# Attention in chunks of 64 tokens, two to a unit, with the work on TensorE in 64x64 tiles

## The chip, the cores and the metric

One core of a Trainium2 chip. The metric is the device time of one execution in microseconds (us). Five engines work side by side on instructions in program order each: TensorE (PE; its weight loads are shown as PEld), VectorE (DVE), ScalarE (ACT), GpSimd (POOL) and SyncE (SP), which here only issues DMA transfers. They wait for each other by semaphores. Matmul results go to PSUM, which has eight banks of 2 KB a partition.

## The reference

A linear attention with a decaying state, then two feed-forward layers on its output:

```
B, H, S, D = 4, 8, 768, 48
state = zeros(B, H, D, D)
for t in range(S):
    cur = einsum('bhd,bhe->bhde', u * k_t, v_t)
    y_t = einsum('bhd,bhde->bhe', r_t, state + cur)
    state = w[:, None] * state + einsum('bhd,bhe->bhde', k_t, v_t)
x = y as (B * S, H * D)                        # 3072 x 384
x = (sigmoid(x @ w_gate) * (x @ w_val)) @ w_out       # inner width 1536
out = relu(x @ w_in)**2 @ w_out2                      # inner width 2048
```

## The kernel before

**Attention.** The 768 tokens are cut into 6 chunks of 128 (index c). A unit n is one chunk of one batch row b, so there are 24 units, n = 4c + b; "chunk 2" below is c = 2. In a unit, the scores of all pairs of tokens are made by matmul (`attn_scores`), from keys and queries that VectorE has multiplied by powers of w (`attn_prep`). `attn_diag` (ScalarE) writes the u term on the diagonal of a score tile `am`, and `attn_mask` (VectorE) copies the scores that count from PSUM into `am`. `attn_out` (TensorE) makes three things: the new contribution `pu` to the state (sums over tokens of scaled key times value; the keys are scaled by `attn_kh`, on GpSimd for c below 3, else on VectorE), the values times the masked scores, and, for c above 0, the state read by the queries. The last two add up in `ya` and `yb`; ScalarE copies them to SBUF, and DMA moves them on to be the input x of the layers. `attn_state` (VectorE) decays the state and adds the copy `us` of `pu`. All matmuls of the attention are fp32. A head has 48 columns, so four heads lie in two halves of the array: an output at PSUM partitions 0 or 64, and for the scores and state reads also an input at partitions 0 or 64.

**Order.** The order on each engine is the order in which the code calls. The four units of chunk 0 run first, while weights and inputs are loaded; `warm` puts matmuls without use between them and 24 behind them, which only keep TensorE busy. Then come the phases of the layers: layer 1 for chunk 0 (its first 7 of 12 inner tiles), for chunks 1 to 5, for the rest of chunk 0, and then layer 2. While layer 1 works on chunk c, the steps of the attention of chunk c+1 are called in between by `fill`, eight steps to a unit (`unit_ops`). So `attn_out` of unit n stands on TensorE between the products `pg` and `pv` of one inner tile, with the scores of unit n+1 at its end. The products are fp32r matmuls of 512 columns, three to one fp32 product. Weights come packed and are converted by ScalarE, VectorE and GpSimd (`convert`) during the first phases.

**Banks of PSUM.** `g` (pg), `v` (pv and also `yb`, which holds half of y and `pu`), `y` (`ya`), `a` (two, scores), `o` (two) and `o2` for the output of a layer.

Of the kernel before, what the change touches and what calls it, by code (L numbers as in the profile page):

```python
# [10 lines left out]
U8 = mybir.dt.uint8  # L11
# [9 lines left out]
C = 128  # L21
# [8 lines left out]
CENT = C // 2  # L30
# [11 lines left out]
def tile_kernel(  # L42
# [28 lines left out]
    anti = cp.tile([C, C], F32, name="anti")  # L71
    mask8 = cp.tile([C, C], U8, name="mask8")
# [3 lines left out]
    trk = cp.tile([DP, HP, C], F32, name="trk")  # L76
# [84 lines left out]
    def tables():  # L161

        R = 32
        e = sp.tile([DP, HP, C], F32, tag="xraw", name="e", bufs=1)
        d0 = sp.tile([DP, HP, R], F32, tag="sig", name="d0", bufs=2)
        d1 = sp.tile([DP, HP, R], F32, tag="sig", name="d1", bufs=2)
        px = cp.tile([DP, HP, 4], F32, name="px")
        f = lambda t: t.rearrange("p h n -> p (h n)")
        q = lambda j, n: px[:, :, j : j + 1].to_broadcast([DP, HP, n])
        pw = sp.tile([DP, HP, R], F32, tag="am", name="pw", bufs=2)  # L170
# [5 lines left out]
            out=f(pw), data0=f(d0), data1=f(d1), initial=0.0, op0=ALU.mult, op1=ALU.add  # L176
        )
        nc.scalar.copy(trk[:, :, CENT : CENT + R], pw)
        nc.vector.tensor_mul(px[:, :, 0], pw[:, :, R - 1], w_sb)
        nc.vector.tensor_mul(px[:, :, 1], px[:, :, 0], px[:, :, 0])  # L180
        nc.vector.reciprocal(px[:, :, 3], px[:, :, 1])
        nc.vector.tensor_mul(trk[:, :, CENT + R :], pw, q(0, R))
        nc.vector.tensor_mul(px[:, :, 2], px[:, :, 1], px[:, :, 1])
        nc.vector.tensor_mul(trk[:, :, 0:CENT], trk[:, :, CENT:], q(3, CENT))
        nc.vector.tensor_mul(e[:, :, 0:CENT], trk[:, :, CENT:], q(1, CENT))
        nc.vector.tensor_mul(e[:, :, CENT:], trk[:, :, CENT:], q(2, CENT))
# [53 lines left out]
    def attn_kh(n):  # L240

        if n >= NU or units[n][0] == NCH - 1:
            return
        k = kv_t[n][:, HD:]
        side(n).tensor_tensor(out=k, in0=k, in1=th, op=ALU.mult)

    def attn_scores(n):
        if n >= NU:
            return
        k, r = k_t[n], r_t[n]  # L250

        pa = pp.tile([C, 2, HP, C], F32, tag="o" if n < B and n % 2 else "a", name="pa")
# [13 lines left out]
        pa_t[n] = pa  # L266

    def attn_mask(n):
        if n >= NU:
            return  # L270
        am, pa = am_t[n].rearrange("p (j r) t -> p r j t", r=2), pa_t.pop(n)
        for p0, t0, t1 in ((0, 64, C), (64, 0, 64)):
            m = mask8[p0:C, t0:t1].unsqueeze(1).unsqueeze(1).to_broadcast([C - p0, 2, HP, t1 - t0])
            nc.vector.copy_predicated(am[p0:C, :, :, t0:t1], m, pa[p0:C, :, :, t0:t1])  # L274

    def attn_out(n):

        c, b = units[n]
        kv, am = kv_t[n], am_t.pop(n)
        ya = pp.tile([P, 2, C], F32, tag="y", name="ya")  # L280
        yb = pp.tile([P, 2 * C + HP * D], F32, tag="v", name="yb")
        pu = yb[:, 2 * C :].rearrange("p (j d) -> p j d", j=HP)
        py = [(yb[:, j // 2 * C : (j // 2 + 1) * C] if j % 2 else ya[:, j // 2]) for j in range(HP)]
        opened = set()

        def mm(out, q, m, bk, lhsT, rhs):

            nc.tensor.matmul(  # L288
                out[64 * q : 64 * q + m],
                lhsT=lhsT,  # L290
                rhs=rhs,
                start=(bk, q) not in opened,
                stop=True,
                skip_group_check=True,
            )
            opened.add((bk, q))


        width = (64, D)
        if c < NCH - 1:  # L300
            for h in range(H):
                q = h % 2
                mm(pu[:, h // 2], q, width[q], 1, kv[:, HD + h * D :][:, : width[q]], kv[:, h * D :][:, :D])
# [4 lines left out]
        if c:  # L308
            for j in range(HP):
                for q in range(2):  # L310
                    o = 64 * (head(q, j) % 2)
# [379 lines left out]
```

## Time and profile before

| | us |
|---|---|
| median of 3 runs | 979.89 (979.03 to 980.71) |
| the profiled execution | 980.53 |
| its span, first to last instruction | 978.7 |
| TensorE busy | 952.3 (97%) |
| VectorE, ScalarE, GpSimd busy | 454.4, 406.9, 128.5 |

The difference of 1.8 us between the execution and its span lies outside of what the trace shows. Busy is the time in which at least one instruction of the engine runs; matmuls overlap each other, so a busy TensorE can still be slow.

### The profile page before, as it was taken

Reading aid. Unit: us, or ns where it says so; the run is one execution under the profiler, and the core shown is the slowest. Engines: PE = TensorE matmul, PEld = TensorE weight load, DVE = VectorE, ACT = ScalarE, POOL = GpSimd, SP = SyncE. Lnnn points to the kernel's source line nnn. Section 1 sums busy time; section 2 is a strip of 40 time slices with the busy share of each in tenths; the row PEclk is TensorE's granted clock in tenths of the full one; section 3 lists DMA queues with packets and bytes.
Section 4 is the critical chain, followed back from the end, with each engine's and each line's share of the span. In section 5 each row is a group of like instructions: output and inputs, shape, how many; then the busy total and the mean of one; then the engine's idle time right before and its main releaser. Section 6 shows DMA issues by size and latency. Waiting matters only on the chain.

```text
span 978.7 us, 13895 instructions
## 1 busy us (share of the span) xinstructions
PE 952.3 (97%) x5544; PEld 758.0 (77%) x5544; DVE 454.4 (46%) x718; ACT 406.9 (42%) x802; POOL 128.5 (13%) x119
## 2 busy tenths in 40 slices
PE   7888999999999999999999999999999999999998
PEld 4566778878888888878888888888888888888886
DVE  7587677643355434323344364333433433433333
ACT  4667656633233234322466463332422322423322
POOL 5467533100000000000133121000000000000000
PEclk7899999999999999999999999999999999999999
DMA  8955554421214122001244440010000100100000
GB/s 309 290 161 156 159 166 149 139 84 54 78 34 137 52 61 85 7 7 37 93 128 128 162 129 1 1 65 1 32 33 1 65 1 1 64 1 1 33 1 32
DMA packets 42224, 76.74 MB, mean 78 GB/s; under 512 B 4912, under 2 KB 17584, under 8 KB 42160
## 3 DMA queue, kind: packets, MB, share of 16 engines
q1 hardware_dynamic: 42160, 75.87, 24.5%
q8 instruction: 43, 0.70, 0.3%
q14 instruction: 21, 0.17, 0.1%
HBM read 60.12 MB, written 11.01 MB: 73 GB/s over the span
## 4 chain that ended last, share of the span: by engine, by line
PE 88%; DVE 4%; ACT 3%; DMA 2%; issue 2%; POOL 1%; SPq 1%; DVEq 0%; ACTq 0%
PE pg L374 35%; PE po L393 19%; PE two L393 16%; PE pv L374 14%; PE ya L288 2%; PE yb L288 2%; DMA first<-in_rkv 1%; PE pa L256 1%; ACT am L238 1%; DVE first L222 1%; DVE raw L155 1%; ACT raw L153 1%; DVE am L274 1%; POOL wu L133 1%; ACT wu L132 0%
## 5 line engine op out<-in xcount | busy, mean ns | idle before, releaser
L374 PE MATMUL pg<-xh,wu 128*128 128x512 f32 x1008 | 316.6, 399 | 9.6 <-ACT xh L361 3.9
L374 PEld LDWEIGHTS pg<-xh,wu 128*128 128x128 f32 x1008 | 190.5, 189 | 58.9 <-ACT xh L361 4.8
L374 PE MATMUL pg<-xl,wu 128*128 128x512 f32 x504 | 195.6, 397 | 0.0
L521 ACT CAST gh<-s 128x512 fp32r<-128x512 f32 (+1 forms) x169 | 105.0, 621 | 207.7 <-DVE s L517 134.3
L393 PE MATMUL po<-gh,wu 128*128 128x512 f32 (+1 forms) x542 | 168.8, 392 | 0.0
L357 DVE TENSOR_TENSOR gl<-s,gh 128x512 fp32r<-128x512 f32 x162 | 114.2, 705 | 88.9 <-PE po L393 57.7
L520 DVE TENSOR_TENSOR s<-s 128x512 f32<-128x512 f32 (+1 forms) x97 | 66.6, 687 | 181.4 <-ACT s L519 181.4
L393 PE MATMUL two<-gh,wu 128*128 128x512 f32 x472 | 147.3, 393 | 0.0
L374 PE MATMUL pv<-xh,wu 128*128 128x512 f32 x432 | 138.4, 401 | 5.7 <-ACT ys L326 5.2
L519 ACT ACTIVATE s<-pg 128x512 f32<-128x512 f32 (+1 forms) x97 | 57.6, 594 | 190.3 <-PE pg L374 190.3
L517 DVE TENSOR_TENSOR s<-pv,s 128x512 f32<-128x512 f32 x72 | 49.7, 691 | 178.4 <-PE pv L374 177.3
L393 PEld LDWEIGHTS po<-gh,wu 128*128 128x128 f32 x542 | 101.6, 188 | 23.9
L374 PEld LDWEIGHTS pg<-xl,wu 128*128 128x128 f32 x504 | 95.4, 189 | 22.5
L393 PE MATMUL po<-gl,wu 128*128 128x512 f32 (+1 forms) x271 | 106.2, 392 | 0.0
L393 PEld LDWEIGHTS two<-gh,wu 128*128 128x128 f32 x472 | 88.5, 188 | 21.3
L374 PEld LDWEIGHTS pv<-xh,wu 128*128 128x128 f32 x432 | 79.5, 188 | 28.1 <-ACT ys L326 8.4
L393 PE MATMUL two<-gl,wu 128*128 128x512 f32 x236 | 92.4, 391 | 0.0
L503 ACT ACTIVATE s<-pg 128x512 f32<-128x512 f32 x72 | 44.0, 612 | 108.5 <-PE pg L374 108.5
L374 PE MATMUL pv<-xl,wu 128*128 128x512 f32 x216 | 84.9, 393 | 0.0
L153 ACT ACTIVATE raw<-raw 128x384 bf16<-128x384 bf16 x68 | 73.5, 1081 | 0.0
L238 ACT ACTIVATE am<-anti,dv 128x128 f32<-128x128 f32 x192 | 60.4, 391 | 15.5 <-DVE dv L228 15.5
L393 PEld LDWEIGHTS po<-gl,wu 128*128 128x128 f32 x271 | 50.8, 187 | 11.3
(295 smaller groups left out, 813.5 us busy)
## 6 DMA issues: line engine op xcount, KB each, us to landing
raw<-in_w SPq DMA_DIRECT2D x68, 384.0 KB, 3.1
kv<-in_rkv SPq DMA_DIRECT2D x16, 384.0 KB, 3.4
xin<-x2d SPq DMA_DIRECT2D x6, 768.0 KB, 4.2
out<-x2s SPq DMA_DIRECT2D x18, 256.0 KB, 2.0
first<-in_rkv SPq DMA_DIRECT2D x16, 256.0 KB, 6.0
kT<-in_rkv SPq DMA_DIRECT2D x16, 256.0 KB, 4.7
rT<-in_rkv SPq DMA_DIRECT2D x16, 256.0 KB, 5.2
x2d<-x2s SPq DMA_DIRECT2D x15, 256.0 KB, 2.0
```

The source lines that it names most:

```text
L133: nc.gpsimd.tensor_tensor(out=w[:, 1], in0=f1, in1=w[:, 0].bitcast(F32), op=ALU.subtract)
L153: nc.scalar.activation(top, top, AF.Prelu, scale=2.0**-112, alpha=2.0**32)
L238: nc.scalar.mul(am_t[n][:, h], anti, dv_t[n][:, h : h + 1])
L288: nc.tensor.matmul(out[64 * q : 64 * q + m], lhsT=lhsT, rhs=rhs, start=(bk, q) not in opened, stop=True, skip_group_check=True,)
L357: (eng or nc.vector).tensor_tensor(out=dst, in0=src, in1=high.bitcast(F32), op=ALU.subtract)
L374: nc.tensor.matmul(ps, lhsT=a, rhs=b_, start=(i == 0), stop=(i == len(pairs) - 1))
L393: nc.tensor.matmul(po[k][:, ts], lhsT=a, rhs=b_[:, ts], start=(first and m == 0), stop=(last and m == 2 and ts is cuts[-1]),)
L503: nc.scalar.activation(s, pg, AF.Sigmoid)
L517: nc.vector.tensor_tensor(out=s[:, ts], in0=pv[:, ts], in1=s[:, ts], op=ALU.mult)
L519: nc.scalar.activation(s[:, ts], pg[:, ts], AF.Relu)
L520: nc.vector.tensor_mul(s[:, ts], s[:, ts], s[:, ts])
L521: nc.scalar.copy(gh[:, ts], s[:, ts])
```

## The change

A unit still has 128 tokens, but they are two chunks of 64 (a = 0 and 1), one behind the other in the recurrence. Scores are made only within a chunk of 64, the state is carried from the first to the second chunk as `mid` (decayed, plus the sums of the first), and the decay tables (`trk`, `th`, `wdec`) are those of 64 tokens. Every matmul of the attention is one of 64 (or 48) rows, at most 64 columns of weights and at most 64 columns of data, so that the array holds four of them at a time. Each of the two heads and each of the two chunks has its own quarter.

The results stand in one tile `att` of three banks: the first and third hold y of the two chunks, the second and third the scores, and the sums stand beside them. Row halves of the array never write one bank at the same time; where the pairing of half and bank changes, `settle` puts a matmul of 8x8 in between. The bank `v` then holds only `pv` and the result of `settle`.

Sums for the state are made one unit ahead: `attn_out` of unit n now makes the values of n, the half of the reads of n whose bank fits, the scores of n+1, the sums of n+1 (`attn_sums`), and the other half of the reads. ScalarE copies the sums of n+1 (`attn_us`, two copies) and then y of n. Sums, `attn_kh` and `mid` are also made in the last chunk; the second half of the state after it is not. In chunk 0 the state was a copy; now it is decayed and added there too. In the start, scores of n+1 stood ahead of `attn_out` of n; now they are inside it.

```diff
-CENT = C // 2
+L = 64
+C = 2 * L
+CENT = L // 2
...
+    att = pp.tile([P, 3, 512], F32, name="att")
+    pa = att[:, 1:3, 0 : HP * L].rearrange("p r (j t) -> p r j t", j=HP)
+    y1, y2 = att[:, 0, 0 : HP * L], att[:, 2, HP * L :]
+    PU = HP * L
+    pu = [att[:, i, PU : PU + HP * D].rearrange("p (j d) -> p j d", j=HP) for i in (1, 0)]
...
+    opened = set()
+    def mm64(bank, q, out, lhsT, rhs):
+        nc.tensor.matmul(
+            out, lhsT=lhsT, rhs=rhs, start=(bank, q) not in opened, stop=True, skip_group_check=True
+        )
+        opened.add((bank, q))
+    def settle(x):
+        tok = pp.tile([P, T], F32, tag="v", name="tok")
+        nc.tensor.matmul(tok[0:8, 0:8], lhsT=x[0:D, 0:8], rhs=x[0:D, 0:8], start=True, stop=True)
     def attn_scores(n):
...
         for j in range(HP):
             for par in range(2):
-                x, z = (slice(64 * i, 64 * i + D) for i in (par, 1 - par))
-                nc.tensor.matmul(
-                    pa[64:C, par, j], lhsT=k[x, j, 64:C], rhs=r[x, j], start=True, stop=True
-                )
-                nc.tensor.matmul(
-                    pa[0:64, 1 - par, j, 64:C],
-                    lhsT=k[z, j, 0:64],
-                    rhs=r[z, j, 64:C],
-                    start=True,
-                    stop=True,
-                )
+                x = slice(64 * par, 64 * par + D)
+                for a in range(2):
+                    t = slice(a * L, (a + 1) * L)
+                    mm64(1 + par, a, pa[64 * a : 64 * a + L, par, j], k[x, j, t], r[x, j, t])
+    def attn_sums(n):
+        if n >= NU:
+            return
+        kv = kv_t[n]
+        settle(kv)
+        for j in range(HP):
+            for q in range(2):
+                h = 2 * j + q
+                for a in range(2):
+                    x = slice(a * L, (a + 1) * L)
+                    mm64(
+                        1 - a,
+                        q,
+                        pu[a][64 * q : 64 * q + width[q], j],
+                        kv[x, HD + h * D :][:, : width[q]],
+                        kv[x, h * D :][:, :D],
+                    )
     def attn_mask(n):
...
-        for p0, t0, t1 in ((0, 64, C), (64, 0, 64)):
-            m = mask8[p0:C, t0:t1].unsqueeze(1).unsqueeze(1).to_broadcast([C - p0, 2, HP, t1 - t0])
-            nc.vector.copy_predicated(am[p0:C, :, :, t0:t1], m, pa[p0:C, :, :, t0:t1])
+        m = mask8.unsqueeze(1).unsqueeze(1).to_broadcast([C, 2, HP, L])
+        nc.vector.copy_predicated(am, m, pa)
+    def attn_us(n):
...
+        us = us_t[n] = sp.tile([DP, 2, HP, D], F32, tag="us", name="us", bufs=2)
+        for a in range(1 if units[n][0] == NCH - 1 else 2):
+            nc.scalar.copy(us[:, a], pu[a][0:DP])
+        if units[n][0] == 0:
+            mid_t[n] = us[:, 0]
     def attn_out(n):
...
+        def reads(second):
+            for j in range(HP):
+                for q in range(2):
+                    h = head(q, j)
+                    a = h % 2 ^ second
+                    o = slice(64 * (h % 2), 64 * (h % 2) + D)
+                    if a or c:
+                        st = mid_t[n][o, j] if a else state[o, b, j]
+                        mm(a, q, j, D, st, r_t[n][o, j, a * L : (a + 1) * L])
         for j in range(HP):
             for q in range(2):
                 h = head(q, j)
-                mm(py[j], q, width[q], j % 2, kv[:, h * D :][:, : width[q]], am[:, h])
...
+                for a in range(2):
+                    x = slice(a * L, (a + 1) * L)
+                    mm(a, q, j, width[q], kv[x, h * D :][:, : width[q]], am[x, h])
+        reads(0)
+        settle(kv)
+        attn_scores(n + 1)
+        attn_sums(n + 1)
+        settle(kv)
+        reads(1)
...
+        attn_us(n + 1)
...
+    def attn_mid(n):
...
+        mid = mid_t[n] = sp.tile([DP, HP, D], F32, tag="mid", name="mid", bufs=2)
+        nc.vector.tensor_mul(mid, state[:, units[n][1]], decay)
+        nc.vector.tensor_add(mid, mid, us_t[n][:, 0])
...
             if late:
-                po[0] = pp.tile([P, T], F32, tag="y", name="po0")
+                po[0] = att[:, 0]
...
-                lambda n=n: attn_mask(n + 1),
+                lambda n=n: (attn_mask(n + 1), attn_mid(n + 1)),
...
         for n in range(B):
-            attn_scores(n + 1)
             attn_pre(n + 2)
             attn_prep(n + 2)
             warm(WARM_OUT[n])
             attn_out(n)
             attn_sum(n + 2)
             attn_mask(n + 1)
+            attn_mid(n + 1)
+            attn_state(n)
```

What this moves on TensorE, first in a unit of chunk 3, from the last matmul of the product pg to the first of pv. Before, with `yb<-kv` the sums, `ya<-am,kv` and `yb<-am,kv` values times scores, `rT,state` the reads, and `pa` the scores of the next unit:

```order
L374 MATMUL pg<-xl,wu 128x512
L288 MATMUL yb<-kv 64x48 [waits DMAHW0_49,DVE_49]
...
L288 MATMUL ya<-am,kv 64x128
L288 MATMUL ya<-am,kv 48x128
L288 MATMUL yb<-am,kv 64x128
...
L288 MATMUL ya<-rT,state 48x128 x2
L288 MATMUL yb<-rT,state 48x128 x2
...
L256 MATMUL pa<-rT,kT 64x128 [waits DMAHW7_49,DMAHW6_49,PE_49]
L259 MATMUL pa<-rT,kT 64x64
...
L374 MATMUL pv<-xh,wu 128x512 [waits PE_49,Activation_49]
```

The same place of the changed kernel, where `tok` is a settle and `att<-kv` a sum:

```order
L429 MATMUL pg<-xl,wu 128x512
L270 MATMUL att<-am,kv 64x64 x2
...
L270 MATMUL att<-rT,mid 48x64 x2
...
L278 MATMUL tok<-kv 8x8 [waits DVE_49]
L270 MATMUL att<-rT,kT 64x64 [waits DMAHW7_49,DMAHW6_49]
L270 MATMUL att<-rT,kT 64x64 x15
L278 MATMUL tok<-kv 8x8 [waits DMAHW4_49,PE_49]
L270 MATMUL att<-kv 64x48 [waits DVE_49]
...
L278 MATMUL tok<-kv 8x8 [waits PE_49]
L270 MATMUL att<-rT,mid 48x64
...
L429 MATMUL pv<-xh,wu 128x512 [waits PE_49]
```

The sums went from the head of the unit, where they were those of unit n, to behind the scores, where they are those of unit n+1; their wait for the engine that scales the keys (here VectorE) moved with them. The wait of pv for ScalarE is gone. Rows of one form that follow each other are counted (x2, x15).

On VectorE in the start, around the mask copy of unit 1 (`am<-mask,pa`) and the conversion of a weight tile behind it, before:

```order
L228 TENSOR_REDUCE dv<-first 128x8 [waits Pool_49]
L274 COPY_PREDICATED am<-mask_70,pa 128x2x4x64 [waits PE_49,Activation_49]
L274 COPY_PREDICATED am<-mask_70,pa 64x2x4x64
L145 SCALAR_TENSOR_TENSOR wt__328<-raw 128x384 [waits DVE_49,Activation_49]
L155 TENSOR_SCALAR raw<-raw 128x384 [waits DMAHW6_49]
```

and in the changed kernel:

```order
L245 TENSOR_REDUCE dv<-first 128x8 [waits Pool_49]
L319 COPY_PREDICATED am<-mask_70,att 128x2x4x64 [waits PE_49,Activation_49]
L397 TENSOR_TENSOR state<-us,wdec 112x192
L398 TENSOR_TENSOR state<-state,us 112x192 [waits DVE_49]
L146 SCALAR_TENSOR_TENSOR wt__376<-raw 128x384
L156 TENSOR_SCALAR raw<-raw 128x384 [waits DMAHW6_49]
```

One mask copy of the two is gone, and the decay and the add of the state of chunk 0 stand in its place.

## Rows read from the trace of the kernel before

**Rows 1.** Stages: span, busy us (x instructions) of PE, PEld, DVE, ACT, POOL; granted clock, DMA.
```profile
42.00:115.00 73.00, 62.31 (x506) 47.25 (x506) 55.13 (x78) 47.28 (x100) 43.54 (x35) 0.93 0.59 181
200.00:290.00 90.00, 90.00 (x655) 72.56 (x654) 41.17 (x72) 30.95 (x74) 0.00 (x0) 1.00 0.23 68
```

**Rows 2.** The chain that ended last, by engine, as shares of the span.
```profile
PE 88%; DVE 4%; ACT 3%; DMA 2%; issue 2%; POOL 1%; SPq 1%; DVEq 0%; ACTq 0%
```

**Rows 3.** TensorE's timeline in unit 14: start, us, what, [idle before].
```profile
241.64 0.39 PE L374 MATMUL pg<-xl,wu 128*128 128x512 f32 x1
241.96 0.61 PE L288 MATMUL yb<-kv 128*64 128x48 f32 x15
...
243.44 0.31 PE L288 MATMUL ya<-rT,state 48*48 48x128 f32 x2
...
243.59 0.28 PE L288 MATMUL ya<-rT,state 48*48 48x128 f32 x2
...
243.70 0.28 PE L288 MATMUL ya<-rT,state 48*48 48x128 f32 x2
...
243.91 0.22 PE L259 MATMUL pa<-rT,kT 48*64 48x64 f32 x1
243.92 0.27 PE L256 MATMUL pa<-rT,kT 48*64 48x128 f32 x1
243.93 0.22 PE L259 MATMUL pa<-rT,kT 48*64 48x64 f32 x1
243.93 0.27 PE L256 MATMUL pa<-rT,kT 48*64 48x128 f32 x1
243.97 0.28 PE L259 MATMUL pa<-rT,kT 48*64 48x64 f32 x3
...
244.58 0.39 PE L256 MATMUL pa<-rT,kT 48*64 48x128 f32 x4
244.90 0.73 PE L374 MATMUL pv<-xh,wu 128*128 128x512 f32 x2
```

**Rows 4.** TensorE's timeline around the first and the last unit of chunk 5.
```profile
379.29 0.86 PE L374 MATMUL pg<-xl,wu 128*128 128x512 f32 x3
...
382.55 0.73 PE L374 MATMUL pv<-xh,wu 128*128 128x512 f32 x2
...
438.00 0.39 PE L374 MATMUL pg<-xl,wu 128*128 128x512 f32 x1
...
440.48 0.73 PE L374 MATMUL pv<-xh,wu 128*128 128x512 f32 x2 [0.49 <-ACT ys L326]
```

**Rows 5.** Groups by line and shape, VectorE: busy us, mean ns | idle before.
```profile
L274 DVE COPY_PREDICATED am<-mask,pa 64x512 f32<-64x512 uint8 x24 | 17.9, 745 | 0.3
...
L342 DVE TENSOR_TENSOR state<-state,wdec 112x192 f32<-112x192 f32 x16 | 8.6, 537 | 0.0
...
L343 DVE TENSOR_TENSOR state<-state,us 112x192 f32<-112x192 f32 x16 | 6.4, 398 | 1.0
```

**Rows 6.** Timelines of TensorE and GpSimd in chunk 1 (42 to 115 us).
```profile
63.32 0.74 PE L374 MATMUL pv<-xh,wu 128*128 128x512 f32 x2 [1.90 <-ACT ys L326]
...
81.08 0.73 PE L374 MATMUL pv<-xh,wu 128*128 128x512 f32 x2
...
80.16 1.32 POOL L245 TENSOR_TENSOR first<-first,th 128x384 f32<-128x384 f32 x1
```

**Rows 7.** Timelines of ScalarE and TensorE in the start; two stages, columns as in rows 1.
```profile
22.24 0.39 ACT L327 COPY ys<-ya 112x256 f32<-112x256 f32 x1
...
32.49 5.35 PE L535 MATMUL pw<-idle 128*128 128x512 bf16 x24
41.70 3.12 PE L374 MATMUL pg<-xh,wu 128*128 128x512 f32 x6 [3.86 <-ACT xh L361]
...
41.28:48.11 6.83, 6.41 (x38) 4.83 (x40) 1.90 (x3) 2.01 (x4) 0.09 (x1) 0.50 0.97 328
91.60:94.05 2.45, 0.00 (x0) 0.00 (x1) 2.45 (x3) 2.45 (x7) 2.45 (x3) 1.00 0.21 30
```

More of the change, by code (lines that the diff above doesn't have):

```diff
@@ L75, in tile_kernel @@
     u_bc = cp.tile([C, H * D], F32, name="u_bc")
[L76 removed]
+    trk = cp.tile([DP, HP, L], F32, name="trk")
     th = cp.tile([C, H * D], F32, name="th")
@@ L175, in tables @@
         nc.vector.tensor_tensor_scan(
-            out=f(pw), data0=f(d0), data1=f(d1), initial=0.0, op0=ALU.mult, op1=ALU.add
+            out=f(p0), data0=f(d0), data1=f(d1), initial=0.0, op0=ALU.mult, op1=ALU.add
         )
-        nc.scalar.copy(trk[:, :, CENT : CENT + R], pw)
-        nc.vector.tensor_mul(px[:, :, 0], pw[:, :, R - 1], w_sb)
+        nc.scalar.copy(pw, p0)
+        nc.vector.tensor_mul(px[:, :, 0], p0[:, :, R - 1], w_sb)
+        nc.vector.reciprocal(px[:, :, 2], px[:, :, 0])
         nc.vector.tensor_mul(px[:, :, 1], px[:, :, 0], px[:, :, 0])
[L181 to L186, printed above, removed]
+        nc.vector.tensor_mul(trk[:, :, 0:CENT], p0, q(2))
+        for i in range(2):
+            pq = px[:, :, i : i + 1].unsqueeze(3).to_broadcast([DP, HP, 2, R])
+            nc.gpsimd.tensor_tensor(
+                out=e[:, :, :, i * R : (i + 1) * R], in0=twice(p0), in1=pq, op=ALU.mult
+            )
         return e, px
     def state_tables(e, px):
-        nc.gpsimd.tensor_copy(wdec, px[:, :, 2])
+        nc.gpsimd.tensor_copy(wdec, px[:, :, 1])
         for par in range(2):
-            pth = pp.tile([C, HP, D], F32, tag="gy"[par], name="pth")
+            pth = pp.tile([C, HP, D], F32, tag="gv"[par], name="pth")
             for j in range(HP):
@@ L279, in attn_out, with mm @@
         kv, am = kv_t[n], am_t.pop(n)
[L280 to L303, printed above, removed]
+        opened.clear()
+        def mm(a, q, j, m, lhsT, rhs):
+            mm64(2 * a, q, (y1, y2)[a][64 * q : 64 * q + m, j * L : (j + 1) * L], lhsT, rhs)
+        def reads(second):
[7 more added lines that the diff above has]
+                        mm(a, q, j, D, st, r_t[n][o, j, a * L : (a + 1) * L])
         for j in range(HP):
@@ L306, in attn_out @@
                 h = head(q, j)
-                mm(py[j], q, width[q], j % 2, kv[:, h * D :][:, : width[q]], am[:, h])
[L308 to L311, printed above, removed]
-                    mm(py[j], q, D, j % 2, state[o : o + D, b, j], r_t[n][o : o + D, j])
-            attn_scores(n + 1)
+                for a in range(2):
[7 more added lines that the diff above has]
+        reads(1)
         while len(kv_t) <= n + (4 if len(kv_t) < IN_W + 2 else 3) and len(kv_t) < NU:
             load_unit(len(kv_t))
+        attn_us(n + 1)
         if b == 0:
@@ L319, in attn_out @@
         ys = bank["y"]
-        if c == 0:
-            nc.scalar.copy(state[:, b], pu[0:DP])
-        elif c < NCH - 1:
-            us = us_t[n] = sp.tile([DP, HP, D], F32, tag="us", name="us", bufs=2)
-            nc.scalar.copy(us, pu[0:DP])
-        two = ys[0:DP, b].rearrange("p (i two) t -> p two i t", two=2)
-        nc.scalar.copy(two[:, 1], yb[0:DP, 0 : 2 * C].rearrange("p (i t) -> p i t", i=2))
-        nc.scalar.copy(two[:, 0], ya[0:DP])
+        for a, y in enumerate((y1, y2)):
+            nc.scalar.copy(ys[0:DP, b, :, a * L : (a + 1) * L], y[0:DP].rearrange("p (j t) -> p j t", j=HP))
         x = xraw[c]
@@ L335, in attn_out @@
             nc.sync.dma_start(out=x[96:128, 2], in_=ys[80:112, :, KT])
+    decay = wdec.unsqueeze(2).to_broadcast([DP, HP, D])
+    def attn_mid(n):
+        if n >= NU or units[n][0] == 0:
+            return
+        mid = mid_t[n] = sp.tile([DP, HP, D], F32, tag="mid", name="mid", bufs=2)
+        nc.vector.tensor_mul(mid, state[:, units[n][1]], decay)
+        nc.vector.tensor_add(mid, mid, us_t[n][:, 0])
     def attn_state(n):
-        b = units[n][1]
-        if n not in us_t:
+        c, b = units[n]
+        us, mid = us_t.pop(n), mid_t.pop(n)
+        if c == NCH - 1:
             return
         st = state[:, b]
-        nc.vector.tensor_mul(st, st, wdec.unsqueeze(2).to_broadcast([DP, HP, D]))
-        nc.vector.tensor_add(st, st, us_t.pop(n))
+        nc.vector.tensor_mul(st, mid, decay)
+        nc.vector.tensor_add(st, st, us[:, 1])
     xs = {}
```

56 lines of the change are left out of this document (33 added, 23 removed).

## The prediction

> **What bounds the kernel now.** I read the stages first, then the chain of work, then short stretches of TensorE's timeline. From 200 to 290 us TensorE is busy for all of the time at the full clock (90.00 of 90.00 us), while VectorE has 41 and ScalarE 31 us of work; from 42 to 115 us no engine is full and TensorE lacks 10.7 us of being busy [rows 1]. The chain that ended last is 88% TensorE [rows 2]. So there are two regimes. In chunks 2 to 5 of the attention (units 8 to 23, from about 115 us) every 0.1 us that a unit holds TensorE is 0.1 us of the run. Before that, VectorE, ScalarE, GpSimd and the DMA queue pass work to each other, and what counts is who is late for whom.
>
> **A unit on TensorE before.** The last projection matmul in front of a unit starts at 241.64, the first behind it (pv) at 244.90: 3.26 us [rows 3]. In it: sums for the state and values times masked scores from 241.96 (1.48), reads of the state from 243.44 (0.47), scores of the next unit from 243.91 (0.99). Each fp32 matmul shows as two passes. The spacings inside give the price of a pass in one tile of the array. The reads run in four 48x48 tiles with 128 columns, and their groups of four start 0.11 apart (243.59, 243.70). The scores of 64 columns (L259) start on one tile at 243.91, 243.97 and 244.03 (the last of its row of three: 243.97 + 0.28 - 0.22): 0.058 for a pass of 64. The last four 128-column passes of the scores end at 244.97, one lasts 0.27, so the last starts at 244.70; pv follows 0.20 later, where a pass takes 0.11: a change of tile shape costs 0.09. The change in front is inside the 0.32 from 241.64 to 241.96. The first pass behind a change has its weights unhidden: 0.15 to the second group of reads instead of 0.11, so 0.04.
>
> **A unit after.** 67 matmuls instead of 40, all but three in 64x64 tiles. Values times scores: 16 matmuls, 32 passes over four tiles, 8 x 0.058 = 0.46. Reads: 8 matmuls of 64 columns in two halves, 4 x 0.056 = 0.22 each (their weights are 48 wide, so I take two thousandths less). Scores and sums: 16 matmuls, 0.46 each. Three 8x8 matmuls (`settle`) lie between, another tile shape each time: out 0.09, two passes with some 0.04 together, in again 0.09, weights 0.04: 0.26 each. Such a matmul stands nowhere in the trace. Its bounds are 0.06 (no change of shape is felt, only two passes of 0.03) and 0.50 (the 0.20 in front of pv twice, and as much again as its passes); I take 0.26, made of the shape changes that the rows show. Sum: 0.32 + 0.04 + 0.46 + 0.22 + 0.26 + 0.46 + 0.26 + 0.46 + 0.26 + 0.22 + 0.09 = 3.05 against 3.26, **0.21 less in each of the 12 units of chunks 2 to 4: 2.5 us**. What the tiles win (1.48 to 0.92, 0.99 to 0.46) goes into the settles (0.78).
>
> In chunk 5 sums are now made too. A unit there took 2.79, from the third pass of its last row of pg (379.29 + 0.86 - 0.39 = 379.76) to pv at 382.55; it will take 3.05: +0.26 three times. The last unit took 2.48, of which 0.49 was pv waiting for ScalarE to empty the bank that y and pv share [rows 4]; with no next unit it takes 0.32 + 0.04 + 0.46 + 0.22 + 0.26 + 0.08 + 0.22 + 0.09 = 1.69, and pv's bank holds no y: -0.79. Together 0.
>
> A rule of the Trainium skill speaks against all this. "TensorE: Matmul & The Clock Gate" (section "Wait — 56ns, not 53.3ns?") says that with hardware decode off the sequencer spends about 62 ns on each MATMUL, which becomes the bound where the array work is shorter. By it the 67 matmuls would take 4.15 us, and the unit would be longer than now. The row of scores does not bear it out: seven passes start between 243.91 and 244.03, 0.020 apart, 0.040 a matmul [rows 3], though they may have been queued.
>
> **Other engines in the dense part.** VectorE loses the half-height mask copy (0.745 us, the second of two a unit) and gains a decay and an add for the middle state (0.537 + 0.398): +0.19 a unit [rows 5]. ScalarE copies the sums twice instead of once; its eight diagonals are half as wide. TensorE hides this while the two have half their time free [rows 1]; on a full engine it would cost the 0.2. ScalarE reaches y only at the end of the unit, 1 us later than now, but its next date is the cast behind pv, 2 us off.
>
> **Chunk 1, 42 to 115 us.** pv no longer waits for the copy of y (1.90 us at 63.32). But sums move up one unit, and with them the need for the scaled keys: GpSimd makes those of unit 7 from 80.16 to 81.48, while unit 6 holds TensorE and its pv starts at 81.08 [rows 6]. Now TensorE stands until 81.5 in front of those sums, and 0.46 + 0.26 + 0.22 + 0.09 follow: pv at 82.5, 1.4 us later. Queued behind on ScalarE are the copies of sums and y and two casts, for which GpSimd and then the next product wait. VectorE gets its mask copy earlier, since scores now end in the middle of a unit. A lost wait of 1.9, a new one of 1.4 and 0.19 more on VectorE per unit: I take 0 for all, bounds -2 (the old wait was on the path, the new one is not) and +3 (the new ones of two units are).
>
> **Prologue.** The DMA queue's next entry waits for y of unit 0, copied at 22.63 [rows 7], and later loads stand behind it. In the new order the values of unit 0 are followed by half its reads, a settle, scores, a settle, sums, a settle and the other reads, 2.4 us of which half was not ahead of y before: some 1.3 us late, and the loads with it. VectorE also decays and adds a state per unit that ScalarE copied before (0.94 less the mask's 0.745, four times: 0.8), and the order inside the unit puts scores behind values (some 0.8 in all). So I expect the first product 1.5 us late (43.2 for 41.70), and the 24 matmuls that only keep TensorE busy, behind the fourth unit, to start near 35.4 instead of 32.49. Their 5.35 us end near 40.8, and TensorE stands idle for 2.4 us, not 3.86. After the 3.86 the clock was at half from 41.28 to 48.11; in the 2.45 us idle before 94.05 it stayed full [rows 7]. If it falls as before, the product starts 1.5 us later and the scores of the unit behind it come 1.3 us earlier within the unit than before: 0 in the chain, which goes on with the mask copy.
>
> **Sum.** -2.5 in chunks 2 to 4, 0 in chunk 5, -0.1 for what chunk 1 passes on of its 0.21 a unit, 0 in the prologue: -2.6. On the profiled 980.53 us (span 978.7) that is 977.9; the median of the runs is 0.64 lower: **977.3 us**.
>
> **Rivals.**
> - *The clock stays full at 42 us.* Six of the first nine matmuls took 3.12 us at half clock [rows 7], so the nine about 4.4; half of that comes back, and 0.7 at the head of the unit behind; with the 1.3 by which its scores come earlier, less the late start of 1.5, the chain is 2.7 us earlier: 974.6. For: the shorter idle time. Against: my 2.4 is a difference of two estimates.
> - *Settles are dearer, or four tiles disturb each other, or the late keys of chunk 1 come through.* 47 settles lie on the path (36, 9 and 2). At 0.29 to 0.45 each: 979 to 986; it turns at 0.31.
> - *Settles are nearly free*, 0.06: 47 x 0.20 more, 968.
> - *TensorE is bound by its instructions.* Reads and scores took 0.47 and 0.99 for 8 and 16 matmuls, 0.059 and 0.062 each, whatever their tiles. If that is a rate of issue, small tiles win nothing: 67 x 0.058 + 0.41 = 4.3 a unit, +1.0 in 12 units, +1.5 in three, +3 in chunk 1: 1000. It turns at 0.042 a matmul. For: two unlike stretches agree. Against: 0.11 for each round of four reads is also what their columns give, and the 0.020 above. The rule quoted is this mechanism; by its 62 ns it would be 1004.
>
> **How the numbers follow.** Forecast 0.36, full clock 0.20, dearer settles or late keys 0.20, issue bound 0.16, free settles 0.05, none of them 0.03. A measurement of this kernel tells about 0.2% (2 us) from no change. Of the forecast's 0.36 I count 0.25 as faster, of the dearer case half within 2 us. Faster 0.25 + 0.20 + 0.05 = 0.50; the same 0.11 + 0.11 + 0.02 = 0.24; slower 0.09 + 0.16 + 0.01 = 0.26. The range leaves out the issue bound and part of the free settles: 970 to 987; the forecast's own is 975 to 980.
>
> **What would show it.** In a unit of chunk 3: 3.05 us from the last pg to the first pv, passes of one tile 0.058 apart, and a hole of 0.26 at each settle. Starts 0.03 apart throughout would be the issue bound. pv without a wait on ScalarE's y; sums with a wait on GpSimd near 80 us; y of unit 0 written 1.3 us later; granted clock between 41 and 48 us at half. TensorE idle behind 200 us would mean a wait that I missed.

## The result: 989.52 us, 0.98% slower, and where the time went

The changed kernel takes 989.52 us (median of 4 runs, 988.94 to 990.49), the kernel before 980.22 us beside it (4 runs, 979.03 to 980.71): ratio 1.0098, 95% interval 1.0080 to 1.0115. The forecast was 977.3 us, in a range from 970 to 987. It was wrong in sign and missed the range.

The profiled execution has a span of 988.7 us, some 10 more than before. The two stages of [rows 1] in the changed kernel, and its chain beside [rows 2]:

```profile
42.00:115.00 73.00, 63.24 (x708) 45.79 (x707) 53.04 (x81) 44.38 (x101) 42.62 (x34) 0.83 0.54 169
200.00:290.00 90.00, 90.00 (x872) 72.30 (x871) 40.51 (x75) 31.52 (x84) 0.00 (x0) 1.00 0.23 72
```

```profile
PE 90%; DVE 4%; ACT 2%; issue 1%; POOL 1%; DMA 1%; SPq 0%; DVEq 0%; ACTq 0%
```

TensorE is as full as before in the dense stage (200 to 290 us). The early stage (42 to 115 us) has a lower granted clock (0.83 for 0.93). A milestone that both traces have is the start of the last pg ahead of a unit's attention on TensorE:

| last pg ahead of | before | after | later by |
|---|---|---|---|
| unit 4 (end of the start) | 45.47 | 51.36 | 5.89 |
| unit 8 (end of chunk 1) | 115.69 | 126.55 | 10.86 |
| from unit 8 to the last matmul's end | 858.35 | 857.10 | -1.25 |

So the start loses 5.9 us, chunk 1 another 5.0 (75.19 us from unit 4 to unit 8 instead of 70.22), and the dense part gives 1.25 back; 0.3 lies behind the last matmul.

**The dense part** went the way that was forecast, by less. TensorE's timeline of unit 14, to be read beside [rows 3]:

```profile
251.44 0.39 PE L429 MATMUL pg<-xl,wu 128*128 128x512 f32 x1
251.76 0.68 PE L270 MATMUL att<-am,kv 64*64 64x64 f32 x32
252.26 0.22 PE L270 MATMUL att<-rT,state 48*48 48x64 f32 x1
...
252.43 0.21 PE L270 MATMUL att<-rT,state 48*48 48x64 f32 x1
...
252.59 0.20 PE L278 MATMUL tok<-kv 48*8 48x8 f32 x2
252.72 0.69 PE L270 MATMUL att<-rT,kT 48*64 48x64 f32 x32
253.35 0.20 PE L278 MATMUL tok<-kv 48*8 48x8 f32 x2
253.48 0.67 PE L270 MATMUL att<-kv 64*64 64x48 f32 x32
254.07 0.20 PE L278 MATMUL tok<-kv 48*8 48x8 f32 x2
...
254.57 0.50 PE L429 MATMUL pv<-xh,wu 128*128 128x512 f32 x1
```

From 251.44 to 254.57 it is 3.13 us (forecast 3.05, before 3.26). The 32 passes of values times scores take 0.50 (251.76 to 252.26), 0.031 for a matmul of two passes, so TensorE is not bound by its instructions. From the start of the last round of reads (252.43) to the first score it is 0.29, of which one round is 0.056.

**The start** shows what failed. TensorE and VectorE, with [idle before] and the releaser; then ScalarE's copies behind unit 0 and the clock of one stretch (columns as in rows 1):

```profile
24.56 0.68 PE L270 MATMUL att<-am,first 64*64 64x64 f32 x32 [0.55 <-DVE am L319]
...
27.37 0.61 PE L590 MATMUL pw<-idle 128*128 128x512 bf16 x2
30.30 1.12 PE L270 MATMUL att<-am,first 64*64 64x64 f32 x32 [2.33 <-DVE am L319]
...
34.85 1.04 PE L590 MATMUL pw<-idle 128*128 128x512 bf16 x2
36.91 1.12 PE L270 MATMUL att<-am,first 64*64 64x64 f32 x32 [1.02 <-DVE am L319]
...
49.42 1.64 PE L429 MATMUL pg<-xh,wu 128*128 128x512 f32 x6
```

```profile
23.78 0.73 DVE L319 COPY_PREDICATED am<-mask,att 128x512 f32<-128x512 uint8 x1 [2.91 <-ACT ys L370]
24.40 0.92 DVE L397 TENSOR_TENSOR state<-us,wdec 112x192 f32<-112x192 f32 x1
25.36 1.05 DVE L398 TENSOR_TENSOR state<-state,us 112x192 f32<-112x192 f32 x1
...
29.54 0.71 DVE L319 COPY_PREDICATED am<-mask,att 128x512 f32<-128x512 uint8 x1
...
36.13 0.72 DVE L319 COPY_PREDICATED am<-mask,att 128x512 f32<-128x512 uint8 x1 [3.59 <-ACT ys L370]
```

```profile
22.66 0.54 ACT L327 COPY us<-att 112x192 f32<-112x192 f32 x2 [4.23 <-PE att L270]
23.09 0.66 ACT L370 COPY ys<-att 112x256 f32<-112x256 f32 x2
```

```profile
29.40:46.46 17.06, 15.14 (x250) 9.83 (x251) 9.27 (x21) 9.85 (x36) 4.32 (x5) 0.50 0.72 232
```

Unit 0 ends on TensorE at 22.55. ScalarE copies the sums made in it and its y until 23.75. Only then, at 23.78, does VectorE start the mask copy of unit 1, whose scores were made inside unit 0; and only behind that copy does unit 1 start, at 24.56. In the code the second half of y (`y2`) and half of the scores (`pa`) share one PSUM bank, and half of the sums shares a bank with the other half. The page "PSUM — Partial Sum Buffer" of the Trainium skill (section "PSUM bank collisions raise a hardware error") says that two engines must not be in one bank at a time and that accesses are to be guarded by bank; the wait on `ys` fits such a guard. Run e3 below shows that it goes when the scores get banks (and a tile) of their own. So the units of chunk 0 run in a ring: TensorE's unit, ScalarE's copies, VectorE's mask (for unit 2 also what VectorE had queued ahead of it), TensorE's next unit. Before, scores stood ahead of the unit in banks of their own and the mask ran beside it. TensorE now stands idle 2.33 us ahead of unit 2, and from 29.40 to 46.46 the granted clock is 0.50, 1.2 GHz: units 2 and 3 take 4.55 us (30.30 to 34.85, 36.91 to 41.46), unit 1 at the full clock 2.81 (24.56 to 27.37). The first product comes at 49.42 instead of 41.70 [rows 7].

**Chunk 1.** What TensorE waited for in all, from 46 to 126 us, how often, and the longest:

```profile
PE pg L429 <- ACT wu L133: 3.7, 3, 2.8
PE att L270 <- POOL first L262: 2.6, 2, 1.4
PE att L270 <- POOL kv L262: 2.3, 1, 2.3
PE pg L429 <- POOL wu L134: 1.9, 3, 0.8
PE pv L429 <- POOL wu L134: 0.4, 1, 0.4
```

The wait of pv for ScalarE's y [rows 6] is gone. Before, it took this much in the same stretch of the kernel:

```profile
PE pv L374 <- ACT ys L326: 4.4, 2, 2.5
```

In its place stand 4.9 us in which the sums wait for the keys that GpSimd scales (L262). The mask waits for y's copy here too. But the waits as such do not add up to the 5.0 us. From unit 4 to unit 8, first before, then in the changed kernel (columns as in rows 1):

```profile
45.47:115.69 70.22, 59.53 (x501) 45.35 (x500) 54.24 (x76) 46.59 (x98) 43.54 (x35) 0.96 0.56 172
51.36:126.55 75.19, 64.27 (x718) 49.18 (x717) 53.78 (x80) 46.08 (x102) 43.96 (x35) 0.86 0.52 161
```

TensorE stands idle for 10.7 and 10.9 us of this; what grew is its busy time, by 4.7, at a lower mean clock. The granted clock was at half (1.2 GHz) from 60.12 to 66.94, from 70.35 to 73.77, from 90.84 to 94.25 and from 101.08 to 107.91, 20.5 us in all, against 6.1 before. Each time it fell within a wait of TensorE or up to 2 us behind one: 2.8 us for converted weights, then 1.15, 1.4 and 2.3 us for keys. No run holds the clock up in this stretch of the changed kernel, so how much of the 5.0 us it made is not shown.

### The profile page after: what moved, and what is told of

Same layout as the page of the kernel before. It is cut to its first block, busy times and chain, and to the rows that moved or that the text cites. A ratio compares the mean times of both kernels' runs of the same rounds, so it can differ in the third digit from the quotient of the medians.

```text
span 988.7 us, 16639 instructions
## 1 busy us (share of the span) xinstructions
PE 961.3 (97%) x6904; PEld 764.3 (77%) x6904; DVE 453.1 (46%) x742; ACT 401.8 (41%) x826; POOL 135.0 (14%) x121
## 4 chain that ended last, share of the span: by engine, by line
PE 90%; DVE 4%; ACT 2%; issue 1%; POOL 1%; DMA 1%; SPq 0%; DVEq 0%; ACTq 0%
PE pg L429 34%; PE two L448 16%; PE pv L429 14%; PE po L448 11%; PE att L448 7%; PE att L270 5%; PE pw L590 1%; PE tok L278 1%; DVE first L239 1%; DMA first<-in_rkv 1%; DVE am L319 1%; ACT am L255 1%; POOL wu L134 0%; DVE raw L156 0%; DVE mid L388 0%
## 5 line engine op out<-in xcount | busy, mean ns | idle before, releaser
L429 PE MATMUL pv<-xh,wu 128*128 128x512 f32 x432 | 141.2, 408 | 0.4 <-POOL wu L134 0.4
L448 PE MATMUL po<-gh,wu 128*128 128x512 f32 (+1 forms) x338 | 105.5, 392 | 0.0
L448 PEld LDWEIGHTS po<-gh,wu 128*128 128x128 f32 x338 | 63.4, 188 | 14.6
L448 PE MATMUL po<-gl,wu 128*128 128x512 f32 (+1 forms) x169 | 66.2, 392 | 0.0
L448 PE MATMUL att<-gh,wu 128*128 128x512 f32 (+1 forms) x204 | 63.4, 392 | 0.0
L255 ACT ACTIVATE am<-anti,dv 128x64 f32<-128x64 f32 x192 | 50.1, 340 | 16.5 <-DVE dv L245 16.5
```

Source lines behind the costliest of these rows:

```text
L255: nc.scalar.mul(am_t[n][:, h], anti, dv_t[n][:, h : h + 1])
L429: nc.tensor.matmul(ps, lhsT=a, rhs=b_, start=(i == 0), stop=(i == len(pairs) - 1))
L448: nc.tensor.matmul(po[k][:, ts], lhsT=a, rhs=b_[:, ts], start=(first and m == 0), stop=(last and m == 2 and ts is cuts[-1]),)
```

## Experiments

Each kernel ran beside the kernel before (979.6 to 980.0 us, and 980.2 beside the changed kernel), on several chips. Gains in the text are differences of medians; by the ratios they differ by up to 0.7 us. The intervals of e1 to e4 overlap that of the changed kernel, those of e1 and e4 most: these two gains alone are not clear of noise. "Unit 4" is the start of the last pg ahead of it, "4 to 8" the stretch to the one ahead of unit 8, both from the profiled execution. Up to unit 3, e6, e9 and e12 are the same code (they differ first in `mid` of unit 4), and yet the first matmul behind unit 3 starts at 33.27, 34.62 and 34.26: one profile's start scatters by over a microsecond. From unit 4 on e8 and e11 are the same code, and their stretches differ by 1.6 us. So both columns count only together with the medians.

| kernel | median us | ratio to before, 95% | unit 4 | 4 to 8 |
|---|---|---|---|---|
| changed kernel | 989.52 | 1.0098 (1.0080 to 1.0115) | 51.36 | 75.19 |
| e1 mask first | 987.41 | 1.0084 (1.0069 to 1.0099) | 51.01 | 72.97 |
| e2 more warm | 986.55 | 1.0074 (1.0059 to 1.0089) | 47.90 | 74.51 |
| e3 scores ahead | 986.43 | 1.0069 (1.0052 to 1.0086) | 47.02 | 76.25 |
| e4 keys early | 988.31 | 1.0082 (1.0067 to 1.0097) | 51.44 | 73.79 |
| e5 settles 64x64 | 977.23 | 0.9973 (0.9963 to 0.9982) | 45.83 | 75.02 |
| e6 = e3 + e4 | 983.94 | 1.0036 (1.0023 to 1.0049) | 45.65 | 72.63 |
| e9 = e6, no mid in chunk 1 | 982.09 | 1.0018 (1.0008 to 1.0027) | 47.67 | 70.50 |
| e12 = e6, mid twice in chunk 1 | 986.68 | 1.0067 (1.0054 to 1.0081) | 49.06 | 75.54 |
| e7 = e6 + e5 | 974.21 | 0.9938 (0.9921 to 0.9954) | 47.58 | 71.92 |
| e8 = e7 + e1 | 974.13 | 0.9937 (0.9923 to 0.9952) | 46.03 | 73.38 |
| e10 = e7, more warm | 973.63 | 0.9933 (0.9918 to 0.9949) | 45.86 | 71.66 |
| e11 = e8, more warm | 973.96 | 0.9937 (0.9923 to 0.9952) | 46.89 | 71.76 |

**e1, the mask ahead of ScalarE's copies.**

```diff
         reads(1)
...
+        attn_mask(n + 1)
         attn_us(n + 1)
...
-                lambda n=n: (attn_mask(n + 1), attn_mid(n + 1)),
+                lambda n=n: attn_mid(n + 1),
...
             attn_sum(n + 2)
-            attn_mask(n + 1)
```

> The only edit to the changed kernel: the mask copy of unit n+1 (VectorE) is called in front of ScalarE's copies of sums and y instead of behind them. Theory (wait): the mask waits for the copy of y because half of y lies in a PSUM bank with half of the scores; without it the mask starts at the end of the unit on TensorE, 1.3 us earlier in each of the units 0 to 7 (for unit 4: 54.6 instead of 55.9 us), VectorE's 21.9 us of idle time in front of the mask ahead of 126 us fall by about 9, and the run becomes 5 to 7 us faster, 983 to 985. Rival (order): what costs is that the scores stand inside the unit at all; then the mask still comes behind the whole unit and the gain is under 2 us, 988 or more. Rival (exchange): sums and y are now copied behind the mask, 0.75 us later, and the next unit or the DMA of y waits for them instead: 989 to 991.

Groups of VectorE ahead of 126 us (busy, mean ns | idle before, releaser): first the changed kernel, then e1.

```profile
L319 DVE COPY_PREDICATED am<-mask,att 128x512 f32<-128x512 uint8 x9 | 6.6, 731 | 21.9 <-ACT ys L370 21.9
```

```profile
L319 DVE COPY_PREDICATED am<-mask,att 128x512 f32<-128x512 uint8 x9 | 6.6, 730 | 18.1 <-PE att L270 18.1
```

And ScalarE's copies in e1, behind unit 0:

```profile
23.57 0.54 ACT L327 COPY us<-att 112x192 f32<-112x192 f32 x2 [6.18 <-DVE am L319]
```

Mask and copies only read these banks, and yet whichever is called second waits for the other: the guard works both ways. The wait on y is gone and the mask now waits for TensorE alone, but the idle time falls by 3.8 us, not 9, and the run by 2.1. In the start nothing is won (51.01): the mask still follows the whole unit, as the rival said, and now y is copied behind the mask. In chunk 1 the stretch is 2.2 us shorter. So the wait for y's copy is real (the trace shows it go), but in the start it is only one piece of the ring.

**e2, the clock.** More matmuls without use between the units:

```diff
-    WARM0, WARM_OUT, WARM_X = 13, (8, 6, 2, 2), 24
+    WARM0, WARM_OUT, WARM_X = 13, (8, 10, 14, 10), 34
```

> The changed kernel with more of the matmuls that only keep TensorE busy in the start: 10, 14 and 10 instead of 6, 2 and 2 in front of units 1 to 3, and 34 instead of 24 behind unit 3. Nothing else moves. Theory (clock): TensorE idles 2.3 and 1.0 us in front of units 2 and 3, and the clock is at half from 29.40 to 46.46 us for it; filled, it stays full there, units 2 and 3 take 2.7 instead of 4.3 us and the first product starts some 3 us earlier: 985 to 986.5. Theory (wait): the loop of mask, unit and copy of y sets the time whatever the clock; units 2 and 3 become shorter only if the clock stays up, and without that the time is that of the changed kernel, 989 to 990. Rival: the matmuls that were added stand in front of units that are ready, and cost up to 2 us: 990 to 992.

TensorE and its clock from 22 to 47 us in e2:

```profile
22.00:47.00 25.00, 24.85 (x430) 14.66 (x429) 18.42 (x31) 17.21 (x56) 14.02 (x12) 1.00 0.77 237
```

The clock stays full and every unit of the start takes 3.11 us from the matmul ahead of it to the one behind. The run is 3.0 us faster and unit 4 comes 3.5 us earlier, though the masks still wait for y's copy in this kernel. So a little more than half of the 5.9 us of the start was paid through the clock: the ring made the idle time, the idle time was followed by 1.2 GHz, and that made the ring itself longer.

**e3, the scores where they stood before the change**, for units 1 to 4, in the free banks `o`:

```diff
+        pa, at = att[:, 1:3], 1
+        if 0 < n <= B:
+            pa, at = pp.tile([P, 2, 512], F32, tag="o", name="pa"), f"o{n}"
...
-        attn_scores(n + 1)
+        if c:
+            attn_scores(n + 1)
...
+            attn_scores(n + 1)
             attn_out(n)
```

> The changed kernel with the scores of units 1 to 4 in front of attn_out of the unit before, as they stood before the change, in the two banks `o` that are free in the start; later units as in the changed kernel. Theory (wait): the mask of unit n+1 then runs beside unit n instead of behind it and behind its y; TensorE no longer waits 2.3 and 1.0 us for masks in chunk 0, its last pg ahead of unit 4 comes near 46 instead of 51.36 us, and the run becomes 5 to 6 us faster, 983 to 985; what chunk 1 loses (5 us between units 4 and 8) stays. Rival (VectorE): the decay and add of the state in chunk 0, about 0.9 us a unit, set the start, and little is won: 988 or more.

VectorE's masks of units 2 to 4:

```profile
25.53 0.74 DVE L325 COPY_PREDICATED am<-mask,pa 128x512 f32<-128x512 uint8 x1 [0.76 <-ACT am L255]
...
29.71 0.73 DVE L325 COPY_PREDICATED am<-mask,pa 128x512 f32<-128x512 uint8 x1 [0.45 <-ACT am L255]
...
35.70 0.71 DVE L325 COPY_PREDICATED am<-mask,pa 128x512 f32<-128x512 uint8 x1
```

No mask of the start waits for y any more: with banks of their own for the scores the wait is gone. Unit 4 comes 4.3 us earlier, the run is 3.1 us faster, less than the 5 to 6 expected. In the profile, 1.1 of what the start won is lost again in chunk 1. The edit does two things at once, banks of their own and scores ahead of the unit; banks of their own with the order kept were not run.

**e4, the keys scaled early.**

```diff
-                lambda n=n: (attn_state(n), attn_pre(n + 2)),
+                lambda n=n: (attn_state(n), attn_pre(n + 2), attn_kh(n + 2)),
...
-                lambda n=n: attn_kh(n + 2),
+                lambda: None,
```

> The changed kernel with GpSimd's scaling of the keys of unit n+2 called directly behind its other two operations for that unit, four steps earlier, from unit 4 on; in the start all stays. Theory (keys): in chunk 1 the sums of unit n+1 wait on TensorE for these keys (4.9 us in the profile of the changed kernel, in units 5, 6 and 7), since GpSimd reaches them behind four or five other operations. Called early they are there in time, the three units fall from 5.50, 4.63 and 6.19 to 3.2 to 3.5 us, and the stretch from unit 4 to unit 8 from 75.2 to 71 or 72 (before the change 70.2): 985 to 987. Rival (converted weights): chunk 1 is bound by the conversion of the weights on ScalarE, VectorE and GpSimd; 1.3 us of GpSimd moved ahead of a conversion only move the wait from the sums to pg or pv, and the stretch stays within 1 us: 988.5 to 990.

TensorE's waits in the same stretch, 46 to 126 us, in e4:

```profile
PE pv L429 <- POOL wu L134: 4.0, 4, 1.6
PE pv L429 <- ACT wu L133: 3.1, 2, 1.6
PE pg L429 <- POOL wu L134: 1.7, 3, 0.8
```

The wait for the keys is gone (4.9 us), and pv now waits 7.1 us for converted weights instead of 0.4. The three units are 3.13 us long, yet the stretch wins only 1.4 and the run 1.2. The mean clock of the stretch is 0.88, little more than 0.86. Both theories said something true: TensorE waited 4.9 us for the late keys, and about a quarter of that reaches the end, since the weights are due next.

**e5, settles that keep the tile shape.**

```diff
-    def settle(x):
+    def settle(x, q=0):
...
-        nc.tensor.matmul(tok[0:8, 0:8], lhsT=x[0:D, 0:8], rhs=x[0:D, 0:8], start=True, stop=True)
+        z = slice(64 * q, 64 * q + 64)
+        nc.tensor.matmul(tok[0:64, 0:8], lhsT=x[z, 0:64], rhs=x[z, 0:8], start=True, stop=True)
...
-        settle(kv)
+        settle(kv, 1)
         for j in range(HP):
```

> The changed kernel with its three settles a unit made as matmuls of a 64x64 tile (64 rows, 64 columns of weights, 8 columns of data) instead of 48x8, so that the tile shape does not change in front of and behind them; each still waits for the one before. Theory (shape): a settle costs 0.26 to 0.29 us because the shape changes twice; it falls to 0.06 to 0.1, so a unit of chunks 2 to 5 takes 2.5 to 2.6 instead of 3.13 us and the run is 8 to 10 us faster, 979.5 to 981.5. Rival (drain): the cost is the ordering itself, whatever the shape, and the unit stays at 3.1 us: 989 to 990.

TensorE around the first settle of a unit of chunk 3 in e5:

```profile
243.10 0.21 PE L270 MATMUL att<-rT,mid 48*48 48x64 f32 x1
243.15 0.17 PE L279 MATMUL tok<-kv 64*64 64x8 f32 x1
243.16 0.28 PE L270 MATMUL att<-rT,kT 48*64 48x64 f32 x3
```

Reads, settle and scores now follow each other without a hole, and the unit takes 2.53 us instead of 3.13: 0.20 less for each settle, 9.0 us in 15 units. The run is 12.3 us faster than the changed kernel (8 to 10 were expected), and faster than before. "TensorEngine Tiling (Array Packing)" of the Trainium skill ("Key Properties") says that a change of tiling mode drains TensorE; this agrees. The first score now starts 0.01 us behind the settle, so the 0.20 us is the price here of two changes of shape together with the emptying of the array between them, which the run does not take apart. The other 3 us go with the start (unit 4 at 45.83), where each unit is a link of the ring and the clock is now at half only from 28.1 to 31.5. In chunk 1 nothing is won: the waits for keys grow to 8.5 us.

**e6 to e8, the parts together.** e6 has the edits of e3 and e4, e7 those of e5 as well, e8 that of e1 too.

> The changed kernel with both: the scores of units 1 to 4 ahead of the unit before, in banks of their own, and the keys scaled early from unit 4 on. If the two waits are what the start and chunk 1 lost, the gains add up (3.1 measured for the scores, 3 to 4 for the keys if that theory holds): 982 to 984, and the rest to before, 3 us and the 1.2 won in the dense part, is the clock and the copies. If the weights bind chunk 1: 986 to 987.

> As the one before, and the settles as matmuls of a 64x64 tile, which took 12.3 us from the changed kernel's time by themselves. If the parts are independent the time is 970 to 972. If the shorter units only wait longer for keys and weights in chunk 1, as units 5 and 7 did with the new settles (6.48 and 7.77 us), part of it is lost again: 974 to 976.

> As the one before, and the mask copy in front of ScalarE's copies of sums and y in every unit. The mask alone gave 2.1 us, most of it in chunk 1 (the stretch from unit 4 to unit 8 took 73.0 instead of 75.2 us) and 0.4 ahead of unit 4, where the scores ahead already take the wait away. If the wait for y's copy in chunk 1 still counts: 1 to 2 us under the kernel before it. If the keys or the weights end later anyway: the same within 0.5.

Scores ahead and early keys together give 5.6 us (3.1 and 1.2 alone): on top of e3 the early keys are worth 2.5, a step that is clear of noise. With the new settles it is 15.3, 2.6 less than e6's 5.6 and e5's 12.3 add up to. The mask first adds nothing to that: with e7's stretch at 71.9 us something else ends last in chunk 1.

**e9 and e12, VectorE in chunk 1.** What remained at e6 was a stretch of 72.6 against 70.2. e9 leaves out the decay and add of `mid` in chunk 1, so the state that came from chunk 0 is missing from the second half of each unit there; e12 makes the two operations twice.

```diff
-        if units[n][0] == 0:
+        if units[n][0] <= 1:
             mid_t[n] = us[:, 0]
...
-        if n >= NU or units[n][0] == 0:
+        if n >= NU or units[n][0] <= 1:
             return
         mid = mid_t[n] = sp.tile([DP, HP, D], F32, tag="mid", name="mid", bufs=2)
```

> The kernel with scores ahead and keys early (983.9 us), without the decay and add of the middle state in the four units of chunk 1: the reads of the second half take the copied sums alone, so that part of the decay of the state is left out. It takes two VectorE operations a unit away, 0.9 to 1.8 us beside GpSimd's work. Theory (VectorE): these are on the chain of mask, state and converted weights in chunk 1 and make up what is still lost there (72.6 us from unit 4 to unit 8 against 70.2 before the change): the stretch falls by 2 or more, 981 to 982.5. Rival (ScalarE and GpSimd set the converted weights): no gain over 0.7, 983 to 984.5.

> The kernel with scores ahead and keys early (983.9 us, ratio to before 1.0036), with the decay and add of the middle state made twice over in each of the four units of chunk 1: two more VectorE operations a unit, 0.9 to 1.8 us. Without them the ratio was 1.0018. Theory (VectorE, in chunk 1, is on the chain): about the same 1.9 us the other way, ratio 1.005 to 1.006, 985 to 986, and the stretch from unit 4 to unit 8 grows from 72.6 to 74 or 75 us. Rival (the 1.9 us was scatter between chips): ratio 1.0025 to 1.0045, 982.5 to 984.5.

Without them 982.09 us and a stretch of 70.50, with them 983.94 and 72.63, with them twice 986.68 and 75.54. The three steps of the ratio (1.0018, 1.0036, 1.0067) go the way of the VectorE theory on both sides, the last a little further than forecast; the stretch of e12 moved by more than the scatter of 1.6 us, that of e9 by little more. The intervals of e9 and e6 overlap a little, that of e12 lies apart from both.

**e10 and e11, more warm matmuls on the combined kernels.**

```diff
-    WARM0, WARM_OUT, WARM_X = 13, (8, 6, 2, 2), 24
+    WARM0, WARM_OUT, WARM_X = 13, (8, 10, 5, 8), 34
```

> The kernel with scores ahead, keys early and settles in 64x64 tiles (974.2 us), with more of the matmuls that keep TensorE busy in the start: 10, 5 and 8 instead of 6, 2 and 2 in front of units 1 to 3 and 34 instead of 24 behind unit 3. In its profile TensorE waits 3.2 us for the first x of the layers and the clock is at half after it. If the clock stays full there, the first nine products take 1.5 to 2.2 us less and the run is 1 to 2 us faster, 972 to 973; if the converted weights of chunk 1 are what ends last, it is the same, 973.5 to 975.

> The same with the mask copy in front of ScalarE's copies (974.1 us without the added matmuls). The clock in the start counts: 972 to 973. The weights count: 973.5 to 975.

Both are the same as without, within the scatter. From unit 4 on e7 and e10 are the same code; the mean clock of their stretches is 0.92 and 0.95, and yet they take 71.92 and 71.66 us, so there a higher clock shortened little. e7, e8, e10 and e11 lie at 973.6 to 974.2 us, 0.6 to 0.7% faster than the kernel before and 1.6% faster than the changed one.

## Why the prediction was wrong, step by step

- **The step that failed: "VectorE gets its mask copy earlier, since scores now end in the middle of a unit"**, and with it the zeros for the prologue and for chunk 1. The scores do end in the middle, but their bank is shared with y, so the mask came behind the unit and behind ScalarE's copies: 21.9 us of VectorE idle ahead of 126 us, all on `ys`. The bank map stood in the change; I counted matmuls in it and not who reads a bank at the same time. No rival had this mechanism.
- **Prologue: 0 forecast, +5.9 measured.** y of unit 0 ended at 23.75 instead of 22.63, 1.1 later (forecast 1.3): right. The 24 matmuls behind the fourth unit were forecast near 35.4, with 0.8 for VectorE's state and 0.8 for the order of the scores; they started at 41.46, since the ring closed. The first product came 7.7 us later, not 1.5. The clock was forecast at half from 41 to 48 us; it was at half from 29.40 to 46.46 and full for that product (six matmuls in 1.64 us, not 3.12). e2 gives the clock's share as 3 to 3.5 us; e3 takes away the ring's cause and gets 4.3 at unit 4.
- **Chunk 1: 0 forecast, bounds -2 and +3; +5.0 measured.** The lost wait of pv was right in kind, but it was 4.4 us in two units, and the sum counted 1.9. The wait for the keys came in three units, 4.9 us, not once with 1.4; 1.2 to 2.5 of it reached the run (e4 alone, and on top of e3). The sum had no term for the clock in this stretch: it was at half for 20.5 us instead of 6.1, and TensorE's busy time grew by 4.7 while its idle time stayed. VectorE was put at +0.19 a unit; the two operations of `mid` took 1.75 (below) where a mask of 0.74 went: +1.0. By e9 and e12 this is worth 2 to 3 us of the run; the forecast took VectorE in chunk 1 as covered by other work, though no engine is full there and each is waited for.
- **A unit in the dense part: 3.05 forecast, 3.13 measured.** Values 0.50, reads 0.22 and the 0.058 for a pass came as forecast. The three settles cost 0.84 against 0.78 (the first: 0.29 from the last round of reads to the scores, less 0.056 for that round, and 0.05 for the slower first pass of the scores, 0.29; the others 0.28 and 0.27), and the change in front of pv 0.11 against 0.09. So -0.13 a unit, not -0.21 (-0.49 in unit 9, which took 3.62 before).
- **Chunk 5: 0 forecast.** Three units took 3.13 (before 2.79) and the last 1.91 (before 2.48): +1.0 - 0.6.
- **Issue bound, 0.16 given:** refuted, 0.031 us a matmul in the values. The rule of 62 ns for a MATMUL with hardware decode off, from the page "TensorE: Matmul & The Clock Gate" of the Trainium skill (section "Wait — 56ns, not 53.3ns?"), does not bind here.
- **Dearer settles**, with late keys: both true in sign, but worth only 2 to 3.5 us together (0.06 a unit, and 1.2 to 2.5 for the keys); they don't explain the result.

Not settled: how the 5.0 us of chunk 1 divide between waits, VectorE and the clock; which engine ends last there once keys, mask and settles are mended (71.7 to 73.4 us against 70.2); and why the start scatters between profiles. A unit without settles was not tried; they are there to keep row halves of the array from writing one bank at the same time.

## What to carry to other kernels

Before a change that lays several results into shared PSUM banks is priced by its matmuls, write down for each bank which engines read it and when: in this kernel a reader of one result waited for the reader of its neighbour, and since scores, copies and the next unit depend on each other the wait closed a ring. Two things are separate in such a ring, the wait and the clock that falls behind it; matmuls without use bought back the second here (3.0 us) while the first stayed. Equal idle time can go with an unequal clock (10.7 and 10.9 us in chunk 1, with 0.96 and 0.86), so read the granted clock of each stretch beside its waits. A matmul that only orders others should keep the tile shape of its neighbours (0.20 us for each here).

## What the runs showed of the hardware

The same small VectorE operation took 0.35 or 1.05 us. In the changed kernel, operations of VectorE and what GpSimd did beside them (it was idle from before 43 to 45.08):

```profile
43.36 0.35 DVE L387 TENSOR_TENSOR mid<-state,wdec 112x192 f32<-112x192 f32 x1
...
56.36 1.02 POOL L134 TENSOR_TENSOR wu<-wt__690,wu 128x384 fp32r<-128x384 f32 x1 [6.22 <-ACT wu L133]
56.54 1.05 DVE L387 TENSOR_TENSOR mid<-state,wdec 112x192 f32<-112x192 f32 x1
...
57.62 0.36 DVE L388 TENSOR_TENSOR mid<-mid,us 112x192 f32<-112x192 f32 x1
```

At 43.36 the decay ran alone. At 56.54 it began while GpSimd worked and ended 0.2 us behind that; the add behind it ran alone again. The averages of the four in chunk 1:

```profile
L388 DVE TENSOR_TENSOR mid<-mid,us 112x192 f32<-112x192 f32 x4 | 3.5, 875 | 0.1
L387 DVE TENSOR_TENSOR mid<-state,wdec 112x192 f32<-112x192 f32 x4 | 3.5, 873 | 0.0
```

That is 1.75 us a unit; the forecast took 0.54 and 0.40 from [rows 5], an average over the run, most of which has no GpSimd beside it [rows 1]. "SBUF — State Buffer" of the Trainium skill ("Who interferes with whom") says that a VectorE instruction with two inputs in SBUF and a GpSimd instruction that reads SBUF exclude each other, whichever comes first; these rows agree.
